# Threshold attention and a maxout FFN in one kernel: the first batch's probabilities go into the products unscaled, and their row scales are multiplied into x^T

## The chip, the cores and the metric

The kernel runs on one core of a Trainium2 chip. The metric is the device time of one execution in microseconds. The core has five engines, each with its own instruction queue that it works off in order: TensorE (PE in the profile, its weight loads PEld) for matrix products, VectorE (DVE), ScalarE (ACT), GpSimd (POOL) and SyncE (SP), which here only issues DMAs. TensorE writes into PSUM, from where VectorE and ScalarE read; POOL works on SBUF alone.

## The reference, cut to what matters

```python
batch, n_heads, seq, head_dim = (8, 8, 576, 64)
n_tokens, d_model, d_ff = (4608, 512, 768)

scores = 1/sqrt(64) * q @ k^T
thresh = max(scores, axis=-1) - tau                      # tau = 0.02
scores = where(scores >= thresh, scores, -1e9)
attn = exp(scores - max(scores))
attn = attn / (sum(attn, axis=-1) + 1e-9)
x = (attn @ v), heads side by side: [8*576, 512]
h = maximum(maximum(x @ w1, x @ w2), x @ w3)             # [4608, 768]
out = h @ w_out                                          # [4608, 512]
```

Everything arrives in float32 and the result is float32. Every score row keeps only the entries that lie within tau of the row's maximum.

## The kernel before, in words

**Tiles.** A "quad" is four heads of one batch; there are 16 of them, two per batch, and `g` counts them, so quads 0 and 1 are the first batch. A quad's rows are cut into 9 chunks of 128 partitions, each with two halves (`r` = 0, 1) of 576 score columns: 288 halves in all. A half is one score tile (token `S`): float32 matmuls into a PSUM bank pair of 1024 columns (`scores`, lines 283 to 305). There are four such PSUM buffers, numbered 0 to 3, shared by all that TensorE does; the digit behind a token names the buffer.

**One half's softmax.** `maximum` (token `m`, line 315) takes the row maximum on VectorE. Then there are two ways, and the string `MASKED` (line 24) chooses one of them for each half. In a masked half VectorE's maximum also writes the negated scores as `z` into SBUF, ScalarE makes the exponential (token `e`), and VectorE multiplies it by a 0/1 mask and sums the row (token `k`, `scalar_tensor_tensor` in `numerators`, line 324). In an unmasked half ScalarE does both steps: a Prelu with a very flat slope (`e`), which reads PSUM, and a second exponential with the row sum (`n`, also in `numerators`). So a masked half has two VectorE passes and one on ScalarE, an unmasked one the reverse. `z` has four buffers for each half.

**From numerators to products.** When both halves of a chunk are summed, VectorE takes the reciprocals of the two sums (token `r`, `reciprocals`, line 332), and POOL multiplies each half of `z` by its row's reciprocal and writes bf16 into `P` (token `p`, `normalized`, line 336). A chunk's P is then turned by one DMA transpose on SP's queue into `ptq` (token `t`, `turned`, line 346); P has six buffers. When a quad is turned, the products `x^T = v^T P^T` run as bf16 matmuls with two column halves side by side (token `O`, `product`, line 352, and `N` for the ninth of the rows that is held apart). `x^T` of a product is copied from PSUM to `xt` as bf16, on VectorE for `r` = 0 (token `w`) and on ScalarE for `r` = 1 (token `x`).

**FFN.** When both quads of a batch are in `xt`, the FFN's passes follow (tokens `F` and `B` for the two halves of a pass over the array's row halves; `h` for the copy on ScalarE and `v` for the maxima on VectorE), and the output products with their copies (`u`) and stores (`o`).

**Side work.** q and k are loaded (`l`), turned by TensorE (`T`), and copied out of PSUM (`a` on ScalarE for q, `c` on VectorE for k); POOL swaps q's row halves (`q`), casts v (`y`) and the FFN weights (`z`, loads `g`).

**The order.** The string `ORDER` (line 40) is the whole program after a written-out beginning (`beginning`, line 672): each letter issues one step, and `_Ordered` (line 82) fixes that each engine keeps the order of issue. So the string decides the queue of every engine. The two first score tiles are issued in the beginning; where tiles are counted here, these two are counted too.

Of the kernel before, what the change touches and what calls it, by code (L numbers as in the profile page):

```python
# [15 lines left out]
OP = AluOpType  # L16
# [8 lines left out]
001110001000100001011000011010010001001000101101001001000000100000011000  # L25
# [15 lines left out]
mmlS2eS3mmleS1mkllnyT0eS3nS2T1alglermpceS0emT1S3knmaqrpkS1elmqpS2rmeS0ypllneS3mnplleT1mretnnmkS2mcgltlzpqS3e  # L41
S0lrpmpeS1etkznenqprnlmpS2S3pmmrmeepS0mnpS2egrpkmpntelS1epmT0kaeerltS3S2tlT0ynmemkeS1nrmpS3ctS2ernnppttT0mlm
pneaS1rtmS3S2pemeS3pqemkmpgneS0rkS1T2qpmqltempyrecpnpS0mqpklS3nemenenS2T1lrpklmerpzapS0pmtryptS3meS2kmeS1S0O
3nnmeempO2NS1eknxrwS0nmeS2rptpqpT3ntmmrnS0tpecmS1pS3eS0tptrmT2S1mmppeatqngleO2ekkleO0rNS3mwxF0elkT2mcnnzpBrp
hS1S2emS0zlpgtpF3F1qemmettkeBqvBS2rnnzF0T3mtBvpnhpkS2meraeF1S0BS3mgevmF2nprS1mepypqBpnF0S3lvkBegF2F1BmhrvS0z
tneBpplzF3nnS2mvBeS1T0mrtT2mhS3pncgpgaS2F0mtBererlmpekvS1emF3S2nntS0pBlemeS1ppzqtS2mvmrF3qentT0pBF1rcmS0pppz
nhenBS3mvO2rmgO1NekglentexnS0F3S1klwmmrnF2plpqypeeBzpBvS0hS1tmF3S2mBtrF1pzpneemrS0vBlneS3mvnS2mrppyS0mnemF1k
S2eS3mreptnepBepmS0F3kpmrS2uutS1kenmnT0arBpekS2emtupueS0mkptpqqO1lltO3emNrlelpkwS2tllxltrlS0F3myF1lmBnpeekph
T2cBF0T3T2vnanqpBS1cvqmF3S2BmneF0hrS1pyperBkF3S2mnBrvmvF0enS1BtS2plmmloppeS3hS0eS1emmtpmF3eekF2BBleF0tlT1vnt
rBvT3aT2haS1pS0kF2crtS3nmBnpmtmF0eS1tqpeeqvBptlmrppF2nveS3lntBmrlF0hS1kpyeBS2mpnvmrenpqyplS3O1qtO0mrNepexkT2  # L50
nS3wF0cS1mrBpmnenS2S1oF3vF0pBtmmeS1pekhlS2toF3rBmmeptynevlT1aBprS2vS0nmmeF1ukketepF3kS1mT2T0rrcBS1ptpqnnaoup
umS0eppmrS2S3mmeeeS0F1eS2qnkpkmT3BS0rnceunrmkmueppS3tlltemO2epO1NotllltS0krwpxS3ppqyF2qnpnmS1BmeS3hF0emmeeF2
BnS1BkrvmnrF3loS0BvpleyyrS2mnpmpphS1ppF0etmS3emllBeF1nF2BtevkrpS0BvS3nS1hmmtleS2lmmetF3tkF0eBpleT1BvrvanT2nF
3cS1BnmF0S2BrhkF3mpeT1vnrBpprveaS0S2nmT1S3pqpncmpS0meeeqmeS1tO2pqmtotlloeO3ltqNF0S1klwBxrpkppS2mrhmF3S0epBmF
2nenS1pvBF0mF3nleBBtottvkS2hF0keF1rurvpmT3BeapkppyrpvS1S2mnS3S0pnemF1mtS3emkS2rpBenepltS0memkmrutpuS2neS3emF
1rmpqkynpS2pqeBemS0uuS2O3kmemekO1NeS0rwT2xoF1olppnT3mnT0BcS2aS3rncqhF0qtF1pBtemmpBkevrF2eS3vlmpnBptnlS0S1S3h
ermmempS2F0ypmF1BBelrteoevnF3T2F0akkqvBBS2nhkymF1pqpnF3verBBS0rvtpmhnS2S1F3mrmlpBpeS0evlmS2eF1pnS3BmnleF2mtl
lvrlttS0eppptyBmS1ehF3lepT2BmltnS0lnltcS1rkvO2O3tmNpmeprT1nnexrapkwS0pqF3qyemT1T2cpBF0S1anepkBS2hvF3S0mreBF1
mekmrnvF2qBeS3vS0unpS2tS1omlrmeppqptlmmnF3pktT0BpecS1eekryuT2uaS0mnS3lomtmrtleF2enpS1kpS3qppnemmS0Bmkerppeue
qS1S0mnurO3kmO1NkwxT0S2eeS1cmpmF3F0kkeBBhF2eF3pvrBS1nnBvpttS0hmemS2mrppF1rpS3BeenmeF0S2vBF1nkvmS3mlnBS0otolh  # L60
F2llterlmF1kBlpypvpBtvteeprS3F0rT2BpS1nnrmpmaS2mtpheS0S3emnF2eT1T0amecBS3ttoS0evyymmS1ppeO2mpqneO3NenqxF0kkt
F1wBT2lolrlklBpS3vphS0cmnF1mtlteS2nqrtBmrpF0vrpqpF3lekBeBpnhF1S2vmT0tlpBS3lS2avmpF0tF1mBrnelekS3evutppmrS2qp
pS1nS0nmF3mrmS1peekenpS2BemmeS0rkS1emuS2tlT0ueT3mcknrannpepF1S0mS3qppBmtotlmlttkrrpeueS0qqmS3lO2ueemoeO0oppt
pkklNwS1lS3xF2mS0BnemehF1kT3mrcnpBS0F2rvS3BltlpnmF1nepmeveS0pkmBS2httnF3eF1mBrBekF0nS2vrBprvpypppS3nmhemeS1S
0F3pF2mmBeBrT1eS0kvnapS3vF1nS2mnBrmmreS3F0pheS1meeBqpnS2mvmeypS1tpS3etlO0qO2mNpmT3neytF1xtlkkrtnweS2ppT0cram
BF3S0BnehvppmeS1rF2qqmT3BF0ncveT3ktnBF2vS1mrnarBhppS0lF3T2qppeBmcS0S1ovmF2mneT3naepBvS0S3enF2mkmrkqpqueenF1n
S2tmS0T3cpqBeupurrS3mmottoS2pS0mttneelotpmS1O3mkkO0rNwrpeexpneF2nkpS0S3S1mBemS0euuppmF1erkS3tltlBptmrF2S0lht
pmeyppBeS1mvO0O3NenmxpS2S1kF0mxemrS3kBF1enF2vBermF0tBhpyppyektBvS1pmF3F2vBkS1BF0nmehS3vrBmtpO2eotpnevO1NkF0S
3krmnrpxpxBhF2S1eBF0mS3F1BnvpmBrS2vS3S0ehemmF1kppmnF2rBvkBF3F0BF1ehBtkvevoF3pptkttO2O0NuprBwS3xS0vmmpeS2ekF1
S3pmF0oeBmrBokettF2peuokoruoF3uhF1pkkF2hvvruF3pF1F2hppF0pvvF3F1vvF2F0F3hvtovhtF1F2F0F3htvF1voF2O0uvO3NvF1xwF  # L70
2hF3F0vF2vhF3F0F2hvF3vvF0F2F3vF0hF2hovF3vF0F2vhF3vvF0vBuuF2BuouoF3uooo
# [31 lines left out]
def kernel(  # L103
# [43 lines left out]
    def weight_loads():  # L147
# [199 lines left out]
    def normalized(c):  # L347
        c["P"] = P = pp.tile([128, W], BF16, name="P")
        for n in range(2):
            pool.tensor_scalar(out=P[:, n * S:(n + 1) * S], in0=c["z", n],  # L350
                                    scalar1=c["rs"][:, n:n + 1], scalar2=1.0, op0=OP.mult, op1=OP.mult)
            if n:
                line["t"].append(c)
# [405 lines left out]
```

## Time and profile before

| what | us |
|---|---|
| median of three runs | 444.31 (444.25 to 444.69) |
| the profiled execution's own time | 443.89 |
| its span, from the first to the last instruction | 442.1 |
| TensorE busy | 421.6 |
| VectorE busy | 401.2 |
| ScalarE busy | 388.1 |
| POOL busy | 320.7 |
| mean granted TensorE clock | 0.988 |

The profile is of one execution. A row of a group or a timeline gives the engine, the operation, the tiles written and read, the shapes, how many there are, and how long they took; the number in square brackets or behind the second bar is how long the engine had been idle before, and what ended that. All instructions carry line 91, the helper that records them, so they are told apart by their tiles. Each float32 matmul of the scores shows as two records. Durations of successive VectorE or ScalarE instructions overlap by some hundredths of a microsecond; the step from one start to the next is what an instruction costs its queue.

### The profile page before, as it was taken

Reading aid. Unit: us, or ns where it says so; the run is one execution under the profiler, and the core shown is the slowest. Engines: PE = TensorE matmul, PEld = TensorE weight load, DVE = VectorE, ACT = ScalarE, POOL = GpSimd, SP = SyncE. Lnnn points to the kernel's source line nnn. Section 1 sums busy time; section 2 is a strip of 40 time slices with the busy share of each in tenths; the row PEclk is TensorE's granted clock in tenths of the full one; section 3 lists DMA queues with packets and bytes.
Section 4 is the critical chain, followed back from the end, with each engine's and each line's share of the span. In section 5 each row is a group of like instructions: output and inputs, shape, how many; then the busy total and the mean of one; then the engine's idle time right before and its main releaser. Section 6 shows DMA issues by size and latency. Waiting matters only on the chain.

```text
span 442.1 us, 14065 instructions
## 1 busy us (share of the span) xinstructions
PE 421.6 (95%) x5193; PEld 306.2 (69%) x5193; DVE 401.2 (91%) x1105; ACT 388.1 (88%) x786; POOL 320.7 (73%) x406
## 2 busy tenths in 40 slices
PE   7777799999999999999999999999999999999995
PEld 6443456767778776867687767867677777777762
DVE  2989999999999999999999999999999999999641
ACT  4998999999999999998999999999999999875422
POOL 3898999899976868586777886677769767554500
PEclk9988899999999999999999999999999999999999
DMA  8999989999999998999999999999999978586602
GB/s 234 301 251 204 243 156 223 284 219 213 224 228 177 241 237 169 202 173 283 178 221 188 242 182 222 166 222 193 236 188 177 247 125 165 100 162 137 176 13 108
DMA packets 212773, 87.44 MB, mean 198 GB/s; under 512 B 185824, under 2 KB 199648, under 8 KB 212704
## 3 DMA queue, kind: packets, MB, share of 16 engines
q1 hardware_dynamic: 212000, 85.69, 95.4%
q8 instruction: 41, 0.67, 0.6%
q10 hardware_dynamic: 704, 0.85, 0.6%
q14 instruction: 28, 0.23, 0.2%
HBM read 34.60 MB, written 9.44 MB: 100 GB/s over the span
## 4 chain that ended last, share of the span: by engine, by line
PE 72%; DVE 6%; ACT 4%; POOL 2%; issue 2%; DMA 1%; SPq 0%; POOLq 0%; DVEq 0%
PE ph L91 29%; PE sc L91 25%; PE po L91 9%; PE o L91 6%; ACT z L91 4%; PE tp L91 3%; DVE z L91 2%; DVE unused L91 2%; POOL P L91 1%; POOL qs L91 1%; DVE kt L91 1%; DMA out_dram<-ob 1%; POOL vb L91 0%; DVE xt L91 0%; DVE hT L91 0%
## 5 line engine op out<-in xcount | busy, mean ns | idle before, releaser
L91 POOL TENSOR_SCALAR P<-z,rs 128x576 bf16<-128x576 f32 x288 | 236.2, 834 | 75.2 <-DVE rs L91 21.8
L91 PE MATMUL sc<-kt,qt 64*128 64x320 f32 (+2 forms) x640 | 183.5, 431 | 4.7 <-ACT z L91 2.6
L91 PE MATMUL sc<-kt,qs 64*128 64x256 f32 (+2 forms) x640 | 181.6, 420 | 4.2 <-ACT z L91 2.1
L91 PE MATMUL ph<-xt,w 64*128 64x288 bf16 (+2 forms) x2160 | 170.7, 283 | 0.4 <-DVE xt L91 0.2
L91 PEld LDWEIGHTS <-w 64*128 64x128 bf16 (+1 forms) x2160 | 125.3, 94 | 33.6 <-issue 6.5
L91 DVE TENSOR_SCALAR_CACHE_REDUCE unused<-sc 128x576 bf16<-128x576 f32 x174 | 128.1, 749 | 4.6 <-PE sc L91 3.6
L91 ACT ACTIVATE z<-sc,nm 128x576 f32<-128x576 f32 x174 | 125.3, 740 | 5.3 <-DVE unused L91 2.9
L91 ACT ACTIVATE z<-z 128x576 f32<-128x576 f32 x174 | 117.7, 681 | 0.2
L91 PEld LDWEIGHTS sc<-kt,qs 64*128 64x128 f32 (+1 forms) x640 | 92.2, 179 | 24.3 <-ACT z L91 4.7
L91 PEld LDWEIGHTS sc<-kt,qt 64*128 64x128 f32 (+1 forms) x640 | 91.9, 179 | 19.4 <-ACT z L91 6.2
L91 DVE SCALAR_TENSOR_TENSOR z<-z 128x576 f32<-128x576 f32 x114 | 95.2, 845 | 0.3
L91 ACT ACTIVATE z<-z,nm 128x576 f32<-128x576 f32 x114 | 86.8, 773 | 4.8 <-DVE z L91 4.5
L91 DVE TENSOR_SCALAR_CACHE_REDUCE z<-sc 128x576 f32<-128x576 f32 x114 | 84.7, 751 | 6.9 <-PE sc L91 3.4
L91 POOL COPY qs<-qt 64x640 f32<-64x640 f32 (+3 forms) x68 | 50.2, 738 | 17.8 <-ACT qt L91 14.1
L91 PE MATMUL po<-wo,hT 64*128 64x512 bf16 (+1 forms) x480 | 53.8, 357 | 0.1
L91 ACT ACTIVATE hm<-ph 128x576 bf16<-128x576 f32 (+2 forms) x54 | 32.2, 595 | 20.7 <-PE ph L91 19.8
L91 DVE TENSOR_TENSOR hm<-ph,hm 128x576 bf16<-128x576 f32 (+2 forms) x54 | 37.0, 684 | 8.8 <-PE ph L91 8.7
L91 PEld LDWEIGHTS <-hT 64*128 64x128 bf16 (+1 forms) x480 | 27.5, 97 | 19.0 <-issue 3.8
L91 DVE TENSOR_TENSOR hT<-ph,hm 128x576 bf16<-128x576 f32 (+2 forms) x54 | 37.2, 688 | 2.6 <-PE ph L91 0.5
L91 PE MATMUL o<-ptq,vb 128*64 128x64 bf16 (+2 forms) x544 | 35.3, 281 | 0.1
L91 ACT ACTIVATION_READ_ACCUMULATOR z<-z 128x1 f32 x174 | 34.5, 198 | 0.0
L91 PEld LDWEIGHTS <-vb 128*64 128x64 bf16 x544 | 21.8, 111 | 15.0 <-issue 5.6
(31 smaller groups left out, 257.2 us busy)
## 6 DMA issues: line engine op xcount, KB each, us to landing
vm<-in_v_dram SPq DMA_DIRECT2D x32, 256.0 KB, 5.1
out_dram<-ob SPq DMA_DIRECT2D x31, 256.0 KB, 2.9
qm<-in_q_dram SPq DMA_DIRECT2D x15, 512.0 KB, 4.5
km<-in_k_dram SPq DMA_DIRECT2D x15, 512.0 KB, 5.4
stage<-in_moe_w_dram SPq DMA_DIRECT2D x9, 512.0 KB, 5.5
ptq<-P SPq DMA_TRANSPOSE x144, 4.1
stage<-in_moe_w_out_dram SPq DMA_DIRECT2D x3, 512.0 KB, 4.4
qm<-in_q_dram SPq DMA_DIRECT2D x16, 64.0 KB, 2.9
```

What stands on the lines that cost most here:

```text
L91: ins = fn(*a, **kw)
```

## The change: what it does

For the quads 0 and 1 the probabilities are not scaled before they are turned. `numerators` writes its bf16 result straight into `P` instead of back into `z`, and its row sum into one column of `sums[g]`, a [128, 18] tile for each of the two quads. POOL's scaling and the 18 small reciprocals of these chunks fall away; one reciprocal per quad (token `R`) makes `scales[g]` from `sums[g]`.

Since x^T has the query rows along its free dimension, the row scales must stand there too. `spread` (token `D`, once for each quad and `r`) does that with TensorE: a float32 matmul of a broadcast scale column (128 rows by 64 equal columns) with the identity lays the 128 scales of a chunk out along the free dimension, equal in 64 partitions; ten such matmuls, eight of 128 columns and two of 64, fill a [128, 576] tile in PSUM. ScalarE copies it to `wide` in SBUF as float32 (token `b`). The copy of x^T out of PSUM becomes, for the first batch, a multiplication by `wide` on VectorE, for both `r` (token `w`; there is no `x` for the first batch).

`wide` takes the place of the buffers that the second batch's `xt` and `hT` use later. `MASKED` is fitted anew in its first row: 16 masked halves of 36 in the first batch instead of 13, and 12 instead of 10 in the second. `ORDER` is fitted anew up to the 125th score tile; behind that both strings issue the same steps in the same order, with the PSUM buffers numbered in another rotation. Up to that point too both issue the same score tiles, turns, products and FFN passes (123 `S`, 28 `T`, 12 `O`, 42 `F`, 40 `B`), 119 `p` against 83, 60 `r` against 42, 43 `k` and 78 `n` against 48 and 73.

```diff
+    sums = [one.tile([128, 18], F32, name=f"sums{x}") for x in range(2)]
+    scales = [one.tile([128, 18], F32, name=f"scales{x}") for x in range(2)]
...
-    def numerators(g, idx, r, zn, sm):
-        acc = sm[:, r:r + 1]
+    def numerators(c, r):
+        g, idx, zn = c["g"], c["idx"], c["z", r]
+        to = zn
+        if g < 2:
+            if "P" not in c:
+                c["P"] = pp.tile([128, W], BF16, name="P")
+            to, acc = c["P"][:, r * S:(r + 1) * S], sums[g][:, 2 * idx + r:2 * idx + r + 1]
+        else:
+            if "sm" not in c:
+                c["sm"] = small.tile([128, 2], F32, name="sm")
+            acc = c["sm"][:, r:r + 1]
         if masked(g, idx, r):
-            vector.scalar_tensor_tensor(out=zn, in0=zn, scalar=thr, in1=zn,
+            vector.scalar_tensor_tensor(out=to, in0=zn, scalar=thr, in1=zn,
                                         op0=OP.is_ge, op1=OP.mult, accum_out=acc)
         else:
-            scalar.activation(out=zn, in_=zn, func=AF.Exp, scale=-1.0 / FLAT, accum_out=acc)
+            scalar.activation(out=to, in_=zn, func=AF.Exp, scale=-1.0 / FLAT, accum_out=acc)
+
+    def spread(g, r, where):
+        ps = bank("d", where)
+        for j in range(5):
+            for i in range(2):
+                idx = 4 if j == 4 else j + 5 * i
+                unit, n = (identf[:, 64 * i:64 * i + 64], 64) if j == 4 else (identf, 128)
+                tensor.matmul(ps[64 * i:64 * i + 64, 128 * j:128 * j + n],
+                              scales[g][:, 2 * idx + r:2 * idx + r + 1].to_broadcast([128, 64]), unit,
+                              start=True, stop=True)
+        line["b"].append(lambda: scalar.activation(out=wide[g, r], in_=ps[:, 0:S], func=AF.Copy))
...
         def on_vector():
-            if part is None:
+            if L["b"] == 0:
+                vector.tensor_tensor(out=dst, in0=ps[:, 0:S], in1=wide[L["qd"], r], op=OP.mult)
+            elif part is None:
                 vector.tensor_copy(out=dst, in_=ps[:, 0:S])
...
-        p.vector = on_vector if part != 1 and r == 0 else None
-        p.scalar = on_scalar if part == 1 or r == 1 else None
+        p.vector = on_vector if L["b"] == 0 or (part != 1 and r == 0) else None
+        p.scalar = None if p.vector else on_scalar
...
+    early = [xp.tile([128, 2, S], F32, name="wide0", tag="xt"), hp_.tile([128, 2, S], F32, name="wide1", tag="hT")]
+    wide = {(x, r): early[x][:, r] for x in range(2) for r in range(2)}
...
+        elif what == "R":
+            g = line["R"].pop(0)
+            assert all(c["halves"] == 2 for c in made[9 * g:9 * g + 9])
+            vector.reciprocal(scales[g], sums[g])
+        elif what == "D":
+            spread(*line["D"].pop(0), where)
+        elif what == "b":
+            line["b"].pop(0)()
```

The order around the products of batch 0 (S, T, O, D and F carry the buffer number). Both lines begin with tile 41, and the `S` behind the dots is tile 49:

```
before: S0 O3 n n m e e m p O2 N S1 e k n x r w S0 ... S1 m m p p e a t q n g l e O2 e k k l e O0 r N S3 m w x F0
after:  S2 T1 n a m m t k k m D3 D1 e b e O3 k t b k k e n e n e k O1 N w S0 w S3 ... S2 l t q D0 e e k n D3 b b e O0 g O3 k r k l p m e n p N y e l p r S1 g w w m n t S0 F2
```

More of the change, by code (lines that the diff above doesn't have):

```diff
@@ L46 @@
[L46 to L55, printed above, removed]
@@ L72 @@
+vvruF2pF0F1hppF3pvvF2F0vvF1F3F2hvtovhtF0F1F3F2htvF0voF1O3uvO2NvF0xwF1hF2F3vF1vhF2F3F1hvF2vvF3F1F2vF3hF1hovF2
+vF3F1vhF2vvF3vBuuF1BuouoF2uooo
 """
@@ L352, in normalized @@
             if n:
-                line["t"].append(c)
+                c["scaled"] = True
             yield
@@ L545, in x_of @@
         if b not in xts:
-            xts[b] = xp.tile([128, 4, S], BF16, name="xt")
+            xts[b] = xp.tile([128, 4, S], BF16, name="xt", tag="xt")
         return xts[b]
@@ L550, in h_of @@
         if b not in hTs:
-            hTs[b] = hp_.tile([128, NF, S], BF16, name="hT")
+            hTs[b] = hp_.tile([128, NF, S], BF16, name="hT", tag="hT")
         return hTs[b]
@@ L594 @@
                 O=products(), F=pieces())
-    line = {k: [] for k in "menkrptahvuxwcqN"}
+    line = {k: [] for k in "menkrptahvuxwcqNb"}
+    line["R"] = [0, 1]
+    line["D"] = [(g, r) for g in range(2) for r in range(2)]
     casts = iter([w[1] for w in wl])
@@ L645, in issue @@
             c, r = line[what].pop(0)
-            if "sm" not in c:
-                c["sm"] = small.tile([128, 2], F32, name="sm")
-            else:
-                c["summed"] = True
-            numerators(c["g"], c["idx"], r, c["z", r], c["sm"])
+            numerators(c, r)
+            c["halves"] = c.get("halves", 0) + 1
         elif what == "r":
-            c = made[line["r"].append(0) or len(line["r"]) - 1]
-            assert c["summed"]
+            c = made[line["r"].append(0) or len(line["r"]) + 17]
+            assert c["halves"] == 2
             reciprocals(c)
@@ L656, in issue @@
         elif what == "t":
-            turned(line["t"].pop(0))
+            c = made[line["t"].append(0) or len(line["t"]) - 1]
+            assert c["halves"] == 2 and (c["g"] < 2 or c["scaled"])
+            turned(c)
+        elif what == "R":
[6 more added lines that the diff above has]
+            line["b"].pop(0)()
         elif what in "ac":
@@ L721 @@
         what = text[x]
-        if what in "STOF":
+        if what in "STOFD":
             x += 1
-        issue(what, int(text[x]) if what in "STOF" else None)
+        issue(what, int(text[x]) if what in "STOFD" else None)
         x += 1
```

52 lines of the change are left out of this document (30 added, 22 removed).

## The prediction

> **What bounds the kernel now.** I read the page first, then the busy time by stretches, then groups and timelines inside 10 to 70 us, where the change lies.
>
> ```profile
> span 442.1 us, 14065 instructions
> PE 421.6 (95%) x5193; PEld 306.2 (69%) x5193; DVE 401.2 (91%) x1105; ACT 388.1 (88%) x786; POOL 320.7 (73%) x406
> ```
>
> ```profile
> 10.00:54.00 44.00, 32.89 (x252) 19.38 (x248) 41.15 (x119) 42.45 (x87) 39.73 (x51) 0.88 1.12 256
> 54.00:70.00 16.00, 14.56 (x176) 8.79 (x174) 15.84 (x43) 15.75 (x34) 15.71 (x19) 1.00 0.83 170
> 70.00:172.00 102.00, 101.45 (x1304) 75.44 (x1302) 98.97 (x272) 98.29 (x201) 87.16 (x106) 1.00 1.09 221
> 172.00:430.00 258.00, 257.70 (x3344) 192.56 (x3339) 240.41 (x662) 224.76 (x454) 175.46 (x223) 1.00 0.94 184
> ...
> 50.00:54.00 4.00, 3.54 (x16) 2.57 (x16) 3.39 (x12) 3.81 (x8) 4.00 (x5) 0.57 1.13 233
> ```
>
> The columns behind the length are the busy time of PE, weight loads, DVE, ACT and POOL, then the granted clock. From 70 to 430 us TensorE idles 0.55 + 0.30 us: it sets the pace, and nothing done there to another engine is worth more than that. Before 54 us it idles 11.1 us, while DVE, ACT and POOL are busy 41, 42 and 40 of 44 us. So the head is softmax pace, the rest is TensorE. What this change is worth is how much sooner (or later) TensorE gets from the head into its full stretch. Both orders agree behind their 125th score tile but for the buffer numbers, and do the same score, product and FFN work before it.
>
> The places by which I date the head are rows of TensorE's timeline: the first products, tile 49, the first FFN pass, tile 52.
>
> ```profile
> 54.30 2.17 PE L91 MATMUL o<-ptq,vb 128*64 128x512 bf16 x32
> ...
> 62.67 0.43 PE L91 MATMUL sc<-kt,qs 64*128 64x256 f32 x1
> ...
> 66.92 0.42 PE L91 MATMUL ph<-xt,w 64*128 64x288 bf16 x4
> 67.59 0.42 PE L91 MATMUL ph<-xt,w 64*128 64x288 bf16 x4 [0.25 <-DVE xt L91]
> ...
> 69.69 0.53 PE L91 MATMUL sc<-kt,qt 64*128 64x320 f32 x1 [0.41 <-DVE kt L91]
> ```
>
> **The change part by part: VectorE.** Its prices are steps from start to start, since an accumulator read overlaps what follows.
>
> ```profile
> 17.15 0.15 DVE L91 RECIPROCAL rs<-sm 128x2 f32<-128x2 f32 x1
> 17.23 0.73 DVE L91 SCALAR_TENSOR_TENSOR z<-z 128x576 f32<-128x576 f32 x1
> 17.89 0.08 DVE L91 DVE_READ_ACCUMULATOR z<-z 128x1 f32 x1
> 17.89 0.75 DVE L91 TENSOR_SCALAR_CACHE_REDUCE z<-sc 128x576 f32<-128x576 f32 x1
> 18.57 0.08 DVE L91 DVE_READ_ACCUMULATOR z<-sc 128x1 f32 x1
> ...
> 33.17 1.65 DVE L91 SCALAR_TENSOR_TENSOR z<-z 128x576 f32<-128x576 f32 x1
> 34.75 0.08 DVE L91 DVE_READ_ACCUMULATOR z<-z 128x1 f32 x1
> ```
>
> A reciprocal steps 0.08 (17.15 to 17.23), a maximum 0.68 (17.89 to 18.57), a masked numerator 0.66 (17.23 to 17.89) when left alone, and 1.58 (33.17 to 34.75) when it starts with a POOL cast:
>
> ```profile
> 33.17 1.03 POOL L91 CAST vb<-vm 128x1024 bf16<-128x1024 f32 x1
> ```
>
> The groups of 10 to 70 us give the means (one duration, then idle before it and its releaser):
>
> ```profile
> L91 DVE SCALAR_TENSOR_TENSOR z<-z 128x576 f32<-128x576 f32 x17 | 17.6, 1039 | 0.0
> L91 DVE TENSOR_SCALAR_CACHE_REDUCE z<-sc 128x576 f32<-128x576 f32 x18 | 13.3, 747 | 2.2 <-POOL P L91 2.2
> L91 DVE COPY kt<-tp 128x640 f32<-128x640 f32 (+1 forms) x6 | 4.5, 743 | 0.0
> L91 DVE CAST xt<-o 128x576 bf16<-128x576 f32 x2 | 1.5, 738 | 0.0
> L91 POOL TENSOR_SCALAR P<-z,rs 128x576 bf16<-128x576 f32 x45 | 36.4, 823 | 3.6 <-DVE rs L91 1.9 <-ACT z L91 0.9
> ```
>
> Taking 0.07 of overlap off (0.73 against the step of 0.66), a masked numerator costs 0.97 in this stretch, 0.31 of it POOL; kt and xt copies cost 0.67.
>
> POOL loses 36 scalings, 36 x 0.823 = 29.6 us. Most of what is left to it before tile 49 is casts, swaps and five scalings of batch 1, some 19 us where it had 49 (counts of the order by the rows' durations). The excess of 0.31 went with a POOL that was 90% busy (39.73 of 44); at 19 of 62 us it is 0.31 x 0.31 / 0.90 = 0.1, so I take 0.75 for a masked numerator (0.66 if POOL never meets it, 0.97 if it meets it as now).
>
> In the trace the 1.58 stands beside a POOL instruction that reads SBUF. The Trainium skill, SBUF — State Buffer, section Who interferes with whom, says that a VectorE instruction with two SBUF inputs contends with a GpSimd instruction that reads SBUF, and that the loser waits for the whole of it. By that rule the new x^T multiply, with one input in PSUM, stays free; the 19 numerators below would lie between 0.66 and 0.97 as the row has it, so the sum keeps its ends.
>
> VectorE's work up to its 46th maximum, about when tile 49 is issued, counted in each order:
> - before: 46 maxima 31.3, 14 masked numerators 13.6, 5 kt 3.4, 21 reciprocals 1.7, 1 xt 0.7: 50.7 us
> - after: 46 maxima 31.3, 19 masked numerators at 0.75 14.3, 5 kt 3.4, some 4 reciprocals 0.3, 2 xt 1.3: 50.6 us
>
> So the masks, which put three more halves of batch 0 on VectorE and move its numerators forward in the queue, spend all that POOL's silence and the reciprocals give: -0.1 us (-1.8 at 0.66, +4.1 at 0.97). The 18-wide reciprocal has no row; its bounds are 0.08 and a full copy of 0.67, twice, so at most 1.2 more. A numerator that writes bf16 into P instead of float32 into z has none either; between nothing and a gain of a half (0.33 a piece, 6 us), I take nothing, as the bf16 and float32 maxima both show 0.75 (745 and 747 ns).
>
> What does go is idle time: the 2.2 us that VectorE waited for POOL to read z, both before 54.1 us. In batch 0 z is now free when its numerator ends. So tile 49 comes at -0.1 - 2.2 = -2.3 us.
>
> **ScalarE** does less, counted to tile 52: five unmasked numerators of some 0.66 less and two x^T copies less, four copies of the spread rows more. Near 0.6 us each that is -3.3 - 1.2 + 2.4 = -2.1, all beside VectorE.
>
> **TensorE.** A score tile is four records of two row halves:
>
> ```profile
> 40.47 0.48 PE L91 MATMUL sc<-kt,qs 64*128 64x256 f32 x1
> 40.47 0.53 PE L91 MATMUL sc<-kt,qt 64*128 64x320 f32 x1
> 40.79 0.38 PE L91 MATMUL sc<-kt,qs 64*128 64x256 f32 x1
> 40.85 0.43 PE L91 MATMUL sc<-kt,qt 64*128 64x320 f32 x1
> 41.00 0.43 PE L91 MATMUL sc<-kt,qs 64*128 64x320 f32 x1
> ```
>
> It takes 0.53 us (40.47 to 41.00) for 2 x (256 + 320) = 1152 columns of float32, 0.46 ns a column with two halves side by side. A spread is 10 float32 matmuls, 8 of 128 and 2 of 64 columns, in two records each: 2304 columns, 1.06 us. Unpaired it is 2.1. I take 1.06, because the products, which use column halves over all 128 rows as the spread does, run paired: 32 in the 2.17 us of the row at 54.30, whose 16 x (512 + 64) columns are 0.235 ns each. Four spreads: 4.2 us (8.5 unpaired).
>
> The loads of their weights I leave under the matmuls: the products' load has a mean of 111 ns, 32 of them 3.6 us, and they do lie under those 2.17 us.
>
> ```profile
> L91 PEld LDWEIGHTS <-vb 128*64 128x64 bf16 x544 | 21.8, 111 | 15.0 <-issue 5.6
> L91 ACT ACTIVATE hm<-ph 128x576 bf16<-128x576 f32 (+2 forms) x54 | 32.2, 595 | 20.7 <-PE ph L91 19.8
> L91 DVE TENSOR_TENSOR hT<-ph,hm 128x576 bf16<-128x576 f32 (+2 forms) x54 | 37.2, 688 | 2.6 <-PE ph L91 0.5
> ```
>
> The Trainium skill speaks against it: TensorE: Matmul & The Clock Gate, Part 3, The mechanism, has weight loads overlap running matmuls only where their row groups differ, and these use all rows. By that rule the products could not do 32 in 2.17 us, so the trace does not bear it out here, though for float32 weights no row shows it; the outcome is the third case below.
>
> The first two spreads stand behind tile 41, ahead of the first products, where TensorE still waits for softmax (11.1 us idle up to 54): hidden. Without that cover they cost 2.1. The other two stand behind tile 49, and there TensorE has little air: from 62.67 to 69.69 us it shows only 0.25 + 0.41 = 0.66 us idle for the same products, FFN pass and tiles. They cost 2.1; the copy that frees the bank for the next product is 0.6 on ScalarE (row hm), and half of it stands out, 0.3; and quad 1's two x^T rows, one each on VectorE and ScalarE before, now run one after the other on VectorE, 0.69 (row hT) for the second, some 0.4 of it behind other matmuls or the tiles between, so 0.3 shows. -0.7 for the idle time: 2.1 + 0.3 + 0.3 - 0.7 = +2.0.
>
> **DMA.** The transposes wait for numerators alone now, not for POOL, but P's six buffers are filled by VectorE and ScalarE, so a late transpose would stop those.
>
> ```profile
> L91 SPq DMA_TRANSPOSE ptq<-P x21: 1242/1352/2905, 16.0 to 69.6; - x21
> DMA to landing us min/median/max: 3.3/4.3/7.0
> ```
>
> At worst five chunks are begun ahead of the issued transposes (the tenth chunk, with five issued). Its buffer hangs on the fourth transpose, some seven numerators back, about 8 us at 1.2 a half: over the 7.0 of the slowest landing. I take nothing. Loads of q, k, v and weights, and what they wait for, keep their number; two weight casts move later, still ahead of their FFN passes.
>
> **Sum.** -2.3 + 2.0 = -0.3 us at tile 52, and behind that TensorE does the same work without idle time. Against the profiled execution, 443.89 us (span 442.1 and 1.8 around it), that is 443.6; this execution lies 0.42 below the median of 444.31, so the median comes to 444.0.
>
> **The rivals.**
> - *The relief in full.* Numerators at 0.66 give another -1.7, and if TensorE's half-rate stretch (0.57 of the clock in 50 to 54) falls into idle time instead of ahead of the first products, up to 1.7 more. Against: POOL keeps casts and swaps. -0.3 - 1.7 = -2.0, with half of the second -2.9: 441.4 to 442.3.
> - *The spread is dear.* Float32 weights over all rows load serially or the halves do not pair: 2.1 us a spread. Then every pair costs 2.1 more; the first still has half its cover: -0.3 + 2.1 + 1.0 = +2.8, 446.8. It decides from 1.2 us a spread up, where the second pair alone takes the gain. For: no float32 matmul in column halves stands in the trace.
> - *Waits trade places.* VectorE, in order, stands at an x^T multiply while the products run late, or the half-rate stretch moves behind 54 us: 4 us at 0.57 is 1.7 us. +1.4, 445.7.
> - *The change does nothing that counts:* VectorE bound as before, spreads in idle time, 444.3; this falls in with the forecast.
>
> **How the numbers follow.** A measurement of this kernel tells about 0.2%, 0.9 us, from no change. Forecast 0.43 (own range 443.0 to 445.1; of it faster 0.10, same 0.29, slower 0.04), relief in full 0.30 (faster 0.28, same 0.02), dear spread 0.15 (slower), waits trade places 0.12 (same 0.03, slower 0.09). Faster 0.38, same 0.34, slower 0.28. The range 441.3 to 446.7 leaves out the ends of the second and third cases, some 0.2.
>
> **What would show it.** Right: masked numerators of 10 to 50 us below 0.85 us mean; no VectorE idle on POOL before 54; a spread near 1.1 us; first products before 53.5 and tile 52 near 69.4; idle of TensorE behind 70 as now. Wrong: numerators still at 1.0; spreads of 2 us; VectorE or ScalarE idle on a DMA of P; a granted clock under 1.00 behind 54 us; TensorE idle over 1 us between 70 and 172, which would mean that another engine took over there.

## The result, and the profile after

The changed kernel took 441.82 us in the median of 9 runs (440.54 to 444.03); the kernel before, timed beside it, 444.31 (443.44 to 444.73, 9 runs). The ratio is 0.994 (95% interval 0.9923 to 0.9957): 2.5 us faster. On another chip, later, 12 runs of the same kernel had a median of 442.99 (441.53 to 445.69) and a ratio of 0.9962 (0.994 to 0.9984). The gain is there both times, and the new kernel's times scatter more than the old one's; a likely source of that is part of what follows.

The page of the profiled execution (442.07 us) and its busy time by the same stretches as before; the columns behind the length are PE, weight loads, DVE, ACT, POOL and then the granted clock:

```profile
span 440.3 us, 14164 instructions
PE 421.6 (96%) x5273; PEld 307.7 (70%) x5273; DVE 400.6 (91%) x1101; ACT 386.1 (88%) x778; POOL 287.1 (65%) x370
```

```profile
10.00:54.00 44.00, 34.63 (x328) 20.63 (x325) 43.20 (x122) 42.45 (x87) 13.46 (x18) 0.96 1.12 250
54.00:70.00 16.00, 14.69 (x188) 10.46 (x190) 14.82 (x41) 14.07 (x29) 13.83 (x17) 1.00 0.86 215
70.00:172.00 102.00, 101.33 (x1316) 75.47 (x1314) 99.09 (x275) 99.57 (x203) 83.13 (x105) 1.00 1.08 221
172.00:430.00 258.00, 257.44 (x3332) 192.09 (x3327) 239.12 (x658) 223.18 (x450) 173.43 (x220) 1.00 0.91 183
```

From 70 us on TensorE is as full as before. The difference is in the first row: POOL fell from 39.73 to 13.46 us, and VectorE now idles 0.80 of the 44 us where it idled 2.85. VectorE's groups of 10 to 70 us, with one mean duration and the idle time before it:

```profile
L91 DVE SCALAR_TENSOR_TENSOR P<-z 128x576 bf16<-128x576 f32 x16 | 12.7, 810 | 0.0
...
L91 DVE TENSOR_SCALAR_CACHE_REDUCE z<-sc 128x576 f32<-128x576 f32 x23 | 16.8, 744 | 0.0
L91 DVE TENSOR_TENSOR xt<-o,wide 128x576 bf16<-128x576 f32 x4 | 2.8, 752 | 0.9 <-PE o L91 0.9
L91 DVE RECIPROCAL scales<-sums 128x18 f32<-128x18 f32 x2 | 0.5, 259 | 0.0
```

A masked numerator of batch 0 takes 810 ns where one of this stretch took 1039, and the 2.2 us that the maxima waited for POOL to read `z` are gone. TensorE's timeline, with the places by which the head was dated: both pairs of spreads, the first products, tile 49, the products of quad 1, tile 52.

```profile
48.64 2.20 PE L91 MATMUL d<-identf,scales 128*64 128x128 f32 x40
50.77 2.38 PE L91 MATMUL o<-ptq,vb 128*64 128x512 bf16 x32
...
59.25 0.48 PE L91 MATMUL sc<-kt,qs 64*128 64x256 f32 x1
...
59.99 2.20 PE L91 MATMUL d<-identf,scales 128*64 128x128 f32 x40
...
62.94 2.14 PE L91 MATMUL o<-ptq,vb 128*64 128x512 bf16 x31 [0.54 <-DMA ptq<-P]
...
68.39 0.53 PE L91 MATMUL sc<-kt,qt 64*128 64x320 f32 x1
```

The first products are 3.5 us earlier (50.77 against 54.30), tile 49 is 3.4 earlier (59.25 against 62.67), tile 52 only 1.3 (68.39 against 69.69). So 2.1 us are given back between tiles 49 and 52. The chain of waits of this stretch (start, length, what) says at what:

```profile
55.35 3.00 ACT z L91 x6
58.35 4.45 DMA ptq<-P
...
62.94 2.57 PE o L91 x24
```

The last transpose of batch 0 is issued at 58.35, when the last numerators are done, and the products wait for it until 62.80.

The starts of some places in the traces of all kernels, each from TensorE's timeline of one profiled execution, with the medians of their runs (the kernel before, timed beside each group of runs, had medians of 444.3 to 444.6):

| kernel | tile 41 | first product | tile 49 | tile 52 | last tile | median |
|---|---|---|---|---|---|---|
| before | 53.6 | 54.3 | 62.7 | 69.7 | 406.6 | 444.3 |
| before_again | 53.8 | 54.5 | 63.1 | 70.0 | 407.4 | 444.4 |
| after | 47.6 | 50.8 | 59.3 | 68.4 | 404.2 | 441.8 |
| after_again | 48.1 | 51.3 | 63.0 | 71.1 | 407.8 | 443.0 |
| old_order | 54.0 | 56.7 | 67.3 | 78.6 | 415.9 | 453.0 |
| old_order_early | 54.0 | 54.8 | 64.8 | 73.0 | 410.6 | 448.5 |
| old_order_new_masks | 53.9 | 54.7 | 64.7 | 72.9 | 410.1 | 447.8 |
| scaled_new_order | 61.3 | 63.0 | 73.9 | 81.6 | 417.5 | 455.2 |
| pool_reads | 57.8 | 61.0 | 69.9 | 78.0 | 414.5 | 452.6 |
| pool_unpaced | 54.2 | 57.3 | 66.5 | 74.6 | 411.1 | 449.5 |
| pool_writes | 64.1 | 68.0 | 76.5 | 84.7 | 421.0 | 457.8 |
| no_first_spreads | 47.6 | 48.6 | 59.3 | 67.4 | 403.9 | 443.9 |
| no_second_spreads | 47.4 | 50.6 | 59.6 | 69.4 | 407.1 | 443.6 |
| turn_early | 46.8 | 50.0 | 58.4 | 66.7 | 403.0 | 442.6 |

### The profile page after: what moved, and what is told of

It reads as the page before. It is cut to its first block, busy times and chain, and to the rows that moved or that the text cites. A ratio compares the mean times of both kernels' runs of the same rounds, so it can differ in the third digit from the quotient of the medians.

```text
span 440.3 us, 14164 instructions
## 1 busy us (share of the span) xinstructions
PE 421.6 (96%) x5273; PEld 307.7 (70%) x5273; DVE 400.6 (91%) x1101; ACT 386.1 (88%) x778; POOL 287.1 (65%) x370
## 4 chain that ended last, share of the span: by engine, by line
PE 74%; DVE 8%; ACT 6%; DMA 5%; issue 3%; POOL 2%; SPq 1%; DVEq 0%; POOLq 0%; ACTq 0%
PE ph L91 29%; PE sc L91 25%; PE po L91 10%; PE o L91 7%; ACT z L91 4%; PE tp L91 3%; DVE unused L91 3%; DMA ptq<-P 3%; DVE P L91 2%; DVE z L91 2%; SPq L91 1%; DMA qm<-in_q_dram 1%; POOL P L91 1%; DMA km<-in_k_dram 1%; DVE kt L91 1%
## 5 line engine op out<-in xcount | busy, mean ns | idle before, releaser
L91 POOL TENSOR_SCALAR P<-z,rs 128x576 bf16<-128x576 f32 x252 | 203.1, 819 | 90.2 <-ACT z L91 34.2
L91 PE MATMUL sc<-kt,qt 64*128 64x320 f32 (+2 forms) x640 | 179.4, 424 | 4.2 <-DVE z L91 1.5
L91 PE MATMUL sc<-kt,qs 64*128 64x256 f32 (+2 forms) x640 | 178.0, 413 | 3.9 <-ACT z L91 1.7
L91 DVE TENSOR_SCALAR_CACHE_REDUCE unused<-sc 128x576 bf16<-128x576 f32 x169 | 124.5, 749 | 4.6 <-PE sc L91 3.9
L91 ACT ACTIVATE z<-sc,nm 128x576 f32<-128x576 f32 x169 | 121.7, 739 | 6.2 <-DVE unused L91 4.1
L91 ACT ACTIVATE z<-z 128x576 f32<-128x576 f32 x149 | 100.9, 681 | 0.3
L91 ACT ACTIVATE z<-z,nm 128x576 f32<-128x576 f32 x119 | 90.4, 772 | 4.5 <-DVE z L91 4.4
L91 DVE TENSOR_SCALAR_CACHE_REDUCE z<-sc 128x576 f32<-128x576 f32 x119 | 88.3, 750 | 5.8 <-PE sc L91 3.2
L91 DVE SCALAR_TENSOR_TENSOR z<-z 128x576 f32<-128x576 f32 x103 | 82.3, 811 | 0.3
L91 ACT ACTIVATION_READ_ACCUMULATOR z<-z 128x1 f32 x149 | 29.6, 198 | 0.0
```

Of the source, the lines that this page charges most:

```text
L91: ins = fn(*a, **kw)
```

## The experiments

**The two halves of the change, one without the other.** `old_order` keeps the old masks and the old order. The first batch's `r` and `p` fall away, and spread and copy stand right before each product:

```diff
-... S0 O3 n n m e e m p O2 N ...
+... S0 D3 b O3 n R n m e e m D2 b O2 N ...
```

> The unscaled P alone: the masks and the order of before, from which the first batch's scalings and small reciprocals are taken out; a spread and its copy stand right before each of the first four products, and both quads' x^T rows are multiplied on VectorE. Relief theory (POOL's silence and the freed z are what pays): VectorE's masked numerators in 10 to 54 us fall from 1.04 to about 0.8 us mean, its idle on POOL goes, so tile 49 comes some 4 us earlier; four spreads of 1.08 with 0.6 of copy behind each, two of them before tile 49, cost 3.4 us per pair, partly in idle time. In all 442 to 443.5 us. Fit theory (the new masks and order are what pays, the unscaled P only makes room for them): not faster than before, 444 to 446 us. Clock theory (fewer half-rate stretches of TensorE): no prediction from the edit; the time follows the number of stretches in the trace, about 1 us for each that falls where TensorE has work.

Measured: 452.98 us (452.19 to 456.42), ratio 1.0196 (1.0162 to 1.0231): 8.7 us slower than before, outside both expectations. `scaled_new_order` is the opposite: new masks, new order, but P scaled by POOL.

```diff
+        if g < 2:
+            rs = scales[g][:, 2 * idx + r:2 * idx + r + 1]
+            vector.reciprocal(rs, acc)
+            pool.tensor_scalar(out=c["P"][:, r * S:(r + 1) * S], in0=zn, scalar1=rs, scalar2=1.0,
+                               op0=OP.mult, op1=OP.mult)
```

> The new masks and the new order alone: P of the first batch is scaled by POOL as before, half by half right behind the numerators (a reciprocal of one column each), no spreads, and x^T is copied out as before on VectorE and ScalarE. Relief theory: 19 masked numerators before tile 49 meet a POOL that is busy as before, so they cost about 1.0 us instead of 0.77 and z is freed late again: tile 49 some 3 to 4 us later than in the changed kernel, less the 2 us that the missing second pair of spreads gives back; 443 to 446 us. Fit theory: the order keeps its gain and the spreads are saved, 440 to 441.5 us.

Measured: 455.18 us (454.77 to 456.72), ratio 1.0244 (1.0213 to 1.0274), also outside both expectations. Two of the waits of TensorE there, between 10 and 72 us (total, times, longest; PEld is its queue of weight loads):

```profile
PE sc L91 <- DVE z L91: 7.4, 10, 1.8
...
PEld sc L91 <- POOL qs L91: 6.5, 2, 4.9
```

Each half alone loses 9 to 11 us; together they gain 2.5. The second run is not quite the old way of scaling (one half at a time, with 36 reciprocals of one column in place of 18 of two), so its size is not the order's alone. What no run tests is an order fitted anew to a P that POOL scales: the new order was fitted to a kernel without that work.

**Was it my placing of the spreads?** In `old_order` TensorE's timeline shows spread, copy and product in series four times:

```profile
54.72 1.21 PE L91 MATMUL d<-identf,scales 128*64 128x128 f32 x20
56.67 1.22 PE L91 MATMUL o<-ptq,vb 128*64 128x512 bf16 x15 [0.75 <-ACT wide L91]
...
59.83 1.18 PE L91 MATMUL o<-ptq,vb 128*64 128x512 bf16 x16 [0.89 <-ACT wide L91]
```

`old_order_early` moves them 35 to 50 steps ahead, and `old_order_new_masks` sets the first batch's masks to the new ones on top:

```diff
-... S0 D3 b O3 n R n m e e m D2 b O2 N ...
+... T2 q m q l t e m D3 y D2 e c b n S0 m q b k l S3 ... S0 O3 n R n m e e m O2 N ...
```

> The unscaled first batch in the old order and with the old masks, as before, but the four spreads and their copies stand well ahead of the products that need them (quad 0's some 50 steps, quad 1's 35 to 50), in PSUM buffers that are unused there, instead of one right before each of the first four products. Theory 'my placing cost it': the 8.7 us that the first such run lost were the chain spread, copy, product in series four times (2 us a time), so 443 to 446 here. Rival 'the old order can't use it': VectorE's saved time turns into idle time and TensorE is as late at tile 41 as before (53.6 us) or later, 446 to 452.

> The same as the run with the spreads placed early, and the first batch's 36 masks are the new ones (16 masked halves instead of 13, the numerator steps of the flipped halves issued in the same places). Theory 'masks': ScalarE was the busier engine of the head (42.45 of 44 us), and only moving halves to VectorE turns its relief into time: 1 to 3 us under the run with the old masks. Rival 'order': the masks alone change less than 1 us; what counts is where the new order issues tiles, numerators and turns.

Measured: 448.45 us (446.52 to 450.03), ratio 1.0084 (1.0061 to 1.0107), and 447.78 (446.16 to 450.54), ratio 1.0078 (1.0053 to 1.0103). The serial spreads had cost 4.5 of the 8.7 us. Behind that the second theory holds: the first batch without POOL's scalings, in the old order, is still 3.3 to 4 us slower than before, and its tile 41 stands at 53.9 to 54.0, within 0.4 us of where it stood. Most of that loss stands behind tile 41 and is the price of the new work: by tile 52 `old_order_early` is 3.3 us behind, and 2.9 of them arise between tiles 41 and 52, where TensorE has the two spreads of quad 1 (1.21 us each, at 58.26 and 60.57) and then waits 1.53 us for x^T (at 70.51). The masks change 0.7 us, less than either kernel's scatter. The busy time of 10 to 54 us, first of `old_order_early`:

```profile
10.00:54.00 44.00, 33.06 (x285) 20.62 (x281) 38.31 (x104) 41.80 (x88) 15.24 (x20) 0.92 1.15 261
```

and of `old_order_new_masks`:

```profile
10.00:54.00 44.00, 31.15 (x290) 18.34 (x286) 40.52 (x110) 41.01 (x82) 15.63 (x21) 1.00 1.13 262
```

POOL is as empty as in the changed kernel, but VectorE idles 5.7 and 3.5 us instead of 0.8: what it saved turned into idle time, since no tile was issued to fill it. The masks alone take some of the idle time away and bring no tile forward.

**What POOL had cost.** Three runs give POOL its load back while nobody reads its results. `pool_reads` and `pool_unpaced` add 36 multiplications of the removed kind and shape to the changed kernel; in the first each waits for its numerator, in the second for nothing. `pool_writes` puts fills that read nothing in their place, at the first one's pace.

```diff
+        if g < 2:
+            pool.tensor_scalar(out=spare.rearrange("p (a u) -> p a u", a=6),
+                               in0=identf[:, None, 0:96].to_broadcast([128, 6, 96]),
+                               scalar1=acc, scalar2=1.0, op0=OP.mult, op1=OP.mult)   # pool_reads
+                               scalar1=one_col, ...)                                 # pool_unpaced
+            pool.tensor_scalar(out=spare[:, 0:1], in0=acc, scalar1=1.0, scalar2=None, op0=OP.mult)
+            for _ in range(2):
+                pool.memset(spare, 1.0)                                              # pool_writes
```

> The changed kernel, in which POOL does 36 more instructions of the removed kind beside it: 576 elements read from SBUF, times the half's row sum, written to a spare tile that nobody reads, each behind the half's numerators. Nothing waits for them but POOL's own later work. Relief theory: the masked numerators go back to about 1.0 us mean in 10 to 54 us (they were 0.81 in the changed kernel), tile 49 comes 2 to 4 us later, 443.5 to 445.5 us in all. Fit theory: VectorE's work is the same and nobody waits for POOL, so 441.8 as the changed kernel.

> As the run with 36 more POOL instructions, but these only write: two fills of 320 elements, about as long together, behind a multiplication of one single column that gives the same pace. If the numerators' cost comes from POOL reading SBUF (the Trainium skill, SBUF — State Buffer, section Who interferes with whom, has an instruction of VectorE with two SBUF inputs contend with a GpSimd instruction that reads SBUF, not with one that only writes), the masked numerators stay near 0.81 us and the time near 441.8. If any POOL work costs VectorE, it is as with the reading instructions: about 1.0 us and 443.5 to 445.5.

> The changed kernel plus 36 POOL multiplications of the removed kind (128x576, float32 in, bf16 out, SBUF alone) in the first batch, as in the run with paced reads, but these wait for nothing, so that POOL works them off as soon as it comes to them, mostly while it would wait for q; its swaps of q are no longer queued behind numerators. Theory 'queue': what cost 10.8 us in the paced runs was the swaps behind operations that wait; without that, 441.8 to 443.5, with masked numerators between 0.81 and 0.95 us and no wait of several us of TensorE for POOL's swaps. Rival 'contention': POOL's reads themselves are what costs; then 445 to 451, with masked numerators at 0.9 us or more and no long wait for a swap.

Measured: 452.63 us (451.69 to 453.89, ratio 1.018, 1.0151 to 1.0208), 457.81 (457.44 to 458.95, ratio 1.0296, 1.0266 to 1.0326), and 449.52 (448.40 to 450.45, ratio 1.0114, 1.0095 to 1.0133). The first two times lie 7 and 12 us above the higher of their expectations. The masked numerators of batch 0 between 10 and 70 us in `pool_reads`:

```profile
L91 DVE SCALAR_TENSOR_TENSOR P<-z 128x576 bf16<-128x576 f32 x16 | 13.9, 883 | 0.0
```

in `pool_writes`:

```profile
L91 DVE SCALAR_TENSOR_TENSOR P<-z 128x576 bf16<-128x576 f32 x16 | 13.0, 825 | 0.0
```

and in `pool_unpaced`:

```profile
L91 DVE SCALAR_TENSOR_TENSOR P<-z 128x576 bf16<-128x576 f32 x16 | 13.8, 878 | 0.0
```

So in the mean POOL's reads hold a masked numerator up by some 70 ns (883 and 878 against 810). The mean hides how it happens: what counts is what a numerator meets when it starts. In the 14 traces, between 10 and 70 us, 113 masked numerators start inside a POOL instruction other than a fill that has more than 0.15 us left. Of these, 104 end 0.59 to 0.62 us after that instruction has ended; beside the other nine it is POOL's instruction that is held up (1.3 to 1.9 us instead of 0.74). The 94 numerators that meet no POOL instruction take 0.74 to 0.76 us. Fills that only write cost a numerator nothing: in `pool_writes` one that starts at 40.50, beside two fills, takes 0.75 us, and the mean of 825 comes from three that start inside a cast or a swap, as the one at 26.46. This is the rule of the Trainium skill, SBUF — State Buffer, section Who interferes with whom, and the trace agrees with it. VectorE's rows in `pool_writes`, then POOL's:

```profile
26.46 1.40 DVE L91 SCALAR_TENSOR_TENSOR P<-z 128x576 bf16<-128x576 f32 x1
...
40.50 0.75 DVE L91 SCALAR_TENSOR_TENSOR P<-z 128x576 bf16<-128x576 f32 x1
```

```profile
26.22 1.04 POOL L91 CAST w<-stage 128x1024 bf16<-128x1024 f32 x1
...
40.49 0.79 POOL L91 MEMSET spare<- 128x320 f32 x2
```

By the means this effect is worth 16 x 0.07 = 1.1 us of the 6.5 to 16 that these kernels lose against the changed one. The kernel whose added POOL work reads next to nothing is even the slowest. What they lose stands in TensorE's waits for POOL's swaps of q. Between 10 and 72 us (total, times, longest) these are, in `pool_reads`:

```profile
PE sc L91 <- POOL qs L91: 8.9, 2, 7.1
```

in `pool_writes`:

```profile
PE sc L91 <- POOL qs L91: 15.6, 3, 9.3
```

and in `pool_unpaced`:

```profile
PE sc L91 <- POOL qs L91: 6.2, 2, 4.5
```

In `after` no matmul waits for a swap there. Tile 52 comes 9.6, 16.3 and 6.2 us later than in `after`, so these waits are nearly the whole loss. The longest one in `pool_unpaced`, with POOL's queue ahead of that swap:

```profile
31.09 0.90 PE L91 MATMUL sc<-kt,qs 64*128 64x320 f32 x1 [4.47 <-POOL qs L91]
```

```profile
24.04 3.63 POOL L91 TENSOR_SCALAR spare<-identf,one_col 128x576 bf16<-128x576 f32 x4
27.63 1.03 POOL L91 CAST w<-stage 128x1024 bf16<-128x1024 f32 x1
28.64 0.74 POOL L91 TENSOR_SCALAR spare<-identf,one_col 128x576 bf16<-128x576 f32 x1
29.33 1.03 POOL L91 CAST vb<-vm 128x1024 bf16<-128x1024 f32 x1
30.42 0.61 POOL L91 COPY qs<-qt 64x512 f32<-64x512 f32 x1
```

In the changed kernel the same swap starts at 23.95:

```profile
23.95 0.61 POOL L91 COPY qs<-qt 64x512 f32<-64x512 f32 x1
```

Even without any wait of their own, the added operations ahead of it make it 6.5 us late; in each of the three kernels 12 of them stand ahead of this swap. My theory for that run had the place right (POOL's queue) and the mechanism half wrong: it is not only that operations wait at the head of the queue; their plain number ahead of a swap is enough. The rival had the time (445 to 451) and the wrong cause, since it denied a long wait for a swap.

**The spreads.** `no_first_spreads` and `no_second_spreads` leave out the spreads and copies of quad 0 and of quad 1, and multiply x^T by a constant instead.

```diff
+        if g == 0:      # no_second_spreads: g == 1
+            line["b"].append(lambda: None)
+            return
```

> The changed kernel without the two spreads of quad 0 and their copies; x^T of quad 0 is multiplied by a constant instead of the row scales, so that part of the computation is left out. If the first pair is hidden in TensorE's waiting for softmax, as predicted: within 0.7 us of the changed kernel, 441.1 to 441.8. If it is not hidden: 2.2 us of spreads and 0.3 of copy less, 439.4.

> The changed kernel without the two spreads of quad 1 and their copies; x^T of quad 1 is multiplied by a constant, so that part of the computation is left out. As predicted, the second pair stands in the way: 2.1 us of spreads and up to 0.3 of copy less, about 439.5. Rival: the products behind it wait for the last DMA transposes anyway (TensorE shows 0.54 us of such a wait behind the spreads), so only 0.5 to 1 us is gained, 441.

Measured: 443.86 us (441.49 to 446.05), ratio 0.9984 (0.9964 to 1.0005), and 443.56 (441.73 to 446.07), ratio 0.9976 (0.9956 to 0.9997). Neither is faster than the changed kernel, and both medians lie outside what was expected. They can't settle the question, because both kernels also do one thing more: POOL fills `wide` (1.06 us, at 0.87) ahead of the identity matrix, and their first score tile starts at 7.58 and 7.30 us, where the other twelve traces have it between 6.40 and 7.07. So the traces have to tell. The first pair is hidden: without it the first product starts 2.1 us earlier (48.64) and tile 49 at 59.25 as in `after`. Without the second pair quad 1's products stand at the transposes instead; the first of their records starts at 60.23, the others after a wait:

```profile
62.87 3.04 PE L91 MATMUL o<-ptq,vb 128*64 128x512 bf16 x31 [2.24 <-DMA ptq<-P]
```

They then take 3.04 us, not 2.14, because TensorE's granted clock falls there; from 64 to 70 us it is 0.72:

```profile
64.00:70.00 6.00, 6.00 (x62) 3.83 (x59) 4.40 (x12) 2.76 (x6) 5.65 (x8) 0.72 0.83 199
```

From these products to tile 52 it is 6.53 us, in `after` 5.45, so some 1.1 us of this trace's stretch between tiles 49 and 52 comes from the clock.

**The last transposes earlier.** `turn_early` issues the turns of the last two chunks right behind their numerators.

```diff
-... k b k k e n e n e k O1 N w S0 w ... T2 m t p l ... a t p z p z
+... k b k k e n t t e n e k O1 N w S0 w ... T2 m p l ... a p z p z
```

> The changed kernel with the transposes of the first batch's last two chunks issued right behind their last numerators, ahead of two loads of v and other steps on SP's queue. In the changed kernel's trace the last one goes out at 58.35 us and lands at 62.8, and the second pair of products waits 0.54 us for it. If that wait is what the products stand at: 0.5 us less and less spread between runs, 441.0 to 441.4. If it is hidden behind the spreads' copies or the x^T rows: 441.8, no change.

Measured: 442.62 us (440.56 to 443.88), ratio 0.9947 (0.993 to 0.9964). In its trace the wait for the transposes is gone and tile 52 stands at 66.7, 1.7 earlier than in `after`; but its median lies between the two of the changed kernel, so no gain can be told.

**Both kernels once more.**

> The kernel before, unchanged, as a second trace of it. Clock theory: another number or place of half-rate stretches of TensorE (three in the first trace, 10.4 us in all), and a time that moves with it by about 1 us a stretch. Relief and fit theory: the same time within 0.2% whatever the stretches, since before 54 us they fall where VectorE and ScalarE set the pace.

> The changed kernel once more, beside the three others on one chip: 440.5 to 444.0 as before, median 441.8 to 442.6. If its median lies near 442.6, the earlier turn of the last chunks gains nothing; if at 441.8 and the profile again shows the products of quad 1 waiting for the last transposes, its spread of times has that place as its likeliest source.

`before_again`: 444.43 us (443.78 to 444.72), ratio 0.999 (0.9979 to 1.0001). Its stretch of 10 to 54 us has the clock 0.88 once more, but between 48 and 54 us it was 1.00 where the first trace of before had 0.72. First `before`, then `before_again`:

```profile
48.00:54.00 6.00, 4.88 (x30) 3.26 (x30) 5.39 (x17) 5.81 (x12) 5.91 (x7) 0.72 1.13 257
```

```profile
48.00:54.00 6.00, 4.12 (x32) 2.19 (x34) 5.72 (x19) 6.00 (x13) 5.59 (x7) 1.00 1.06 237
```

The first product starts at 54.30 in the one and at 54.51 in the other: the half-rate stretch ahead of it costs nothing there, as TensorE waits for softmax either way.

`after_again`: 442.99 us, as told above. Its profiled execution took 445.1 us, 3 more than that of `after`, and shows where such a difference comes from. Up to the first products it is within 0.6 us of `after`; then its chain of waits has

```profile
44.92 8.24 DMA ptq<-P
...
58.92 2.20 PE sc L91 x16
...
63.66 2.13 PE d L91 x40
```

and VectorE's timeline

```profile
53.25 0.76 DVE L91 SCALAR_TENSOR_TENSOR P<-z 128x576 bf16<-128x576 f32 x1 [1.77 <-DMA ptq<-P]
```

A numerator that writes into `P` waits until the transpose issued at 44.92 has given that buffer back, 8.2 us later, and everything in VectorE's queue stands behind it. SP's queue in that stretch shows four transposes in one row, 2.4 us each:

```profile
47.82 9.76 SPq L91 DMA_TRANSPOSE ptq<-P  x4
```

The second cause is on the same chain. The 16 score records at 58.92 take 2.20 us; the same 16 take 1.25 in `turn_early`. TensorE's granted clock is low there:

```profile
58.00:60.00 2.00, 1.63 (x22) 1.24 (x22) 2.00 (x8) 1.83 (x3) 2.00 (x4) 0.73 0.72 142
60.00:62.00 2.00, 2.00 (x22) 1.22 (x16) 1.87 (x7) 1.20 (x4) 2.00 (x3) 0.50 1.06 249
```

Tile 49 comes at 62.96, 3.7 us later than in `after`. Of these, 0.6 had been lost up to the first products, 1.8 are lost up to the tile at 58.92 (56.51 in `after`), where the wait of 1.77 lies, and 1.3 behind it, where TensorE has no wait: the way to tile 49 takes 4.04 us at the lower clock and 2.74 in `after`. Now the second pair of spreads is on the chain too.

## Why the prediction was right or wrong, point by point

The range held the time. The likeliest forecast (444.0) was 2.2 us too slow, and the time is that of the first rival, the relief in full (441.4 to 442.3); the later median of 442.99 lies between the two. That rival's own reasons are not what happened: numerators did not fall to 0.66 (their step is 0.810 - 0.07 = 0.74, the 0.75 of the forecast), and its second term, the half-rate stretch falling into idle time, is worth nothing ahead of the first products, as the two traces of before show. So the agreement with that rival is luck. In `old_order_new_masks` the clock was 1.00 throughout the head, and tile 41 still stood at 53.9.

- *Where it is decided.* Right. From tile 52 to the last tile all 14 traces take 335.9 to 337.7 us, so a kernel keeps what it has lost or gained there to within 1.8 us. "The same work without idle time" was off by a little: the five traces with the old order average 337.3, the nine with the new one 336.45. Some 0.9 us of the gain therefore lies behind tile 52, and 0.6 of that before tile 125, where the two strings still issue different steps. What makes it there stays open.
- *Masked numerator 0.97 to 0.75, no waiting of the maxima for POOL.* The numbers are right, 0.74 and 0.0, but the working behind 0.75 is not: I scaled the excess of 0.31 us by POOL's busy share. In `pool_unpaced` POOL is busy 40.62 of 44 us, more than before, and a numerator takes 878 ns, not 1039. What decides is how many numerators start inside a POOL instruction that reads SBUF.
- *VectorE's work -0.1, so tile 49 at -2.3.* Too small for `after` (-3.4) and `turn_early` (-4.2); in `after_again` the tile comes 0.3 us later than before, for the two causes told above. The count of work was the wrong tool: I took VectorE's idle time, but for the POOL waits, as given. In the new order VectorE idles 0.80 us in 44, in the old order with the same relief 3.5 to 5.7.
- *POOL's part.* This is the missing term. I priced POOL as a neighbour that slows VectorE (0.31 us a numerator, the 2.2 us of waits), not as a queue of its own. Putting 36 operations back into that queue, 12 of them ahead of one swap of q, delays that swap by 6.5 us and more and costs TensorE 4.5 to 9.3 us at one place. The new order, which asks for its tiles 5 to 6 us earlier (tile 41 at 47.6 instead of 53.6), stands or falls with that queue being empty. The neighbour effect is there and is worth about 1.1 us by the means.
- *A spread 1.06 us.* Right: 2.20 for a pair, 1.10 each, with column halves paired and the weight loads underneath; the dear spread is out. (Its price was summed wrongly: 444.31 + 2.8 is 447.1, not 446.8.) The trace does not bear out the rule that I cited beside it either (the Trainium skill, TensorE: Matmul & The Clock Gate, Part 3, The mechanism): these float32 matmuls use all 128 rows, and with loads in series a pair would have shown 4.2.
- *First pair hidden.* Right, by the trace of `no_first_spreads`.
- *Second pair +2.0 between tiles 49 and 52.* The number came in `after` (9.14 against 7.02 us, +2.1), but by luck. In the six other traces that have the new order and this pair, the stretch takes 8.13 to 8.24 us, +1.1 to +1.2, so the term was too large by about 0.8. The other 1.0 us in `after` is the wait for the last transposes, which I had put at nothing. Without the pair the stretch takes 9.80 us, some 1.1 of it through the clock; the products then stand at the transposes.
- *DMA: "I take nothing".* This is the step that failed on the other side, a term put at nothing. I counted that the tenth chunk's buffer hangs on a transpose some 8 us back and set that against a landing of 7.0. The time to landing of the transposes issued between 36 and 68 us in `after`:

```profile
DMA to landing us min/median/max: 3.0/4.5/7.7
```

and in `after_again`:

```profile
DMA to landing us min/median/max: 2.9/4.0/8.5
```

The slowest is longer than the one I had taken from the trace of before, and SP's queue stands ahead of the landing. In `after` the last transpose is 4.45 us of the chain, in `after_again` VectorE stands 1.77 us at a buffer of P. In that execution this wait and the half-rate stretch behind it take back all that the head had gained: 445.1 us. The profiled execution of `no_second_spreads` (445.0) has both as well, waits of 0.42 and 2.24 us for transposes and then the lower clock. In those of `after`, `no_first_spreads` and `turn_early` (442.1, 441.5 and 440.6) no engine waits more than 0.54 us for a transpose between 36 and 72 us, and the clock is 1.00 from 54 to 70. So I hold the two together for the likeliest source of the new kernel's scatter (440.5 to 445.7 over 21 runs). Whether the wait brings on the half-rate stretch is not shown, and the mean clock alone does not order the runs: the two slowest of the 21 have the lowest (0.990 and 0.987), but 444.03 and 444.96 us came with 0.995 and 0.994.
- *Waits trade places.* This rival's price (445.7) is what the longer executions of the new kernel come to (445.1 in the profiled one), and half of its mechanism is what happened there: the half-rate stretch moved behind 54 us and cost 1.3 us, where the rival had 1.7. The other half is P's buffers in the place of the x^T multiply; VectorE's wait at that is 0.9 us (group `xt<-o,wide` above), 0.8 in `after_again`.

The sum that the runs give for `after` against `before`: tile 49 -3.4, then +1.1 for the second pair and +1.0 for the last transposes, behind tile 52 -1.1, together -2.4 at the last tile. What stays open is how the -3.4 divides between fewer waits and the order: of the two halves as they were run, neither works without the other.

## What to carry to other kernels

Relief of an engine that is not the last to finish becomes time only where the order has something ready to put into the gap; try a mechanism and the order fitted to it separately before you credit either. An in-order engine's cost is not its busy share but what stands behind its operations: look for the one transfer or swap queued behind the work that is to be removed. A buffer ring that was drained by an engine's own pace becomes a ring drained by a DMA when the step between is taken out, and then a late landing can set the time of an execution.

## What the runs showed of the hardware that I had not expected

- A masked numerator that starts inside a POOL instruction that reads SBUF ends about 0.6 us after it, whatever the instruction (104 of 113 cases in 14 traces); one that starts first takes its usual 0.75 us. POOL fills that only write leave it at 0.75. Yet the fills made the slower kernel: with their one-column steps they took longer in POOL's queue (70 of 364 ns and 35 of 298 ns, 35.9 us) than 36 multiplications of 849 ns (30.6 us).

```profile
L91 POOL MEMSET spare<- 128x320 f32 x70 | 25.5, 364 | 4.1
L91 POOL TENSOR_SCALAR spare<-sums 128x1 f32<-128x1 f32 x35 | 10.4, 298 | 7.2 <-DVE P L91 4.6
```

```profile
L91 POOL TENSOR_SCALAR spare<-identf,sums 128x576 bf16<-128x576 f32 x36 | 30.6, 849 | 10.6 <-DVE P L91 5.8 <-ACT P L91 1.5 <-DMA ptq<-P 0.8
```

- The half-rate stretches of TensorE's clock lie in different places in two executions of one kernel (0.72 and 1.00 between 48 and 54 us) with the same mean of 0.88 over the head, and move no tile there by more than 0.4 us. In `after_again` one lies between 58 and 63 us, where TensorE has no wait, and costs 1.3 us.
- A reciprocal of 18 columns takes 259 ns on VectorE, near the lower of the bounds that I gave (0.08 and 0.67).
